# Scores of two of four batches as two float32r products over 128 rows, and P V placed with the next pair's scores

## The chip, the cores and the metric

The kernel runs on one core of one Trainium2 chip. The metric is the device time of one execution in microseconds, the median of three runs. A core has TensorE (PE in the rows, with PEld for its weight loads), VectorE (DVE), ScalarE (ACT), GpSimd (POOL) and SyncE, whose queue (SP, SPq) issues the transfers between HBM and the on-chip SBUF. TensorE writes into PSUM, in banks of 128 x 512 float32.

## What is computed

Block-causal attention for 4 batches, 8 heads, 576 tokens and a head size of 64, then two MLPs over the 2304 tokens: 512 to 1536 (a gate and a value) to 512, and 512 to 2048 to 512.

```python
scores = scale * np.matmul(q, k.transpose(0, 1, 3, 2))
mask = block_i >= block_j          # blocks of 64 tokens
scores = np.where(mask, scores, -1000000000.0)
attn = np.exp(scores - np.max(scores, axis=-1, keepdims=True))
attn = attn / (np.sum(attn, axis=-1, keepdims=True) + 1e-09)
x = np.matmul(attn, v)             # heads side by side: 2304 x 512
x = (1.0 / (1.0 + np.exp(-(x @ w_gate))) * (x @ w_val)) @ w_out
h = x @ w_in
out = np.maximum(0.01 * h, h) @ w_out2
```

## The kernel before

**The plan.** The kernel first collects all operations in a `Plan`: each has an engine, a cost, a due time, the tokens that it reads and writes, and the buffers that it uses. `order()` then simulates the engines with these costs. Whenever an engine is free it takes, of the operations whose inputs and buffers are there, the one that is due first; on TensorE an operation of the same `kind` as the last one counts as due 1.0 earlier (`GAIN`). The result is one program order for each engine. On the chip each engine, the SP queue too, works strictly in that order and waits by semaphore. Buffers come from `Ring`s: the n-th tile of a ring with k buffers waits until tile n-k has had all its users, and the tiles of a ring are taken in order.

**Float32 from float32r.** The MLP products and their weights are split: a value is its rounded copy in float32r (hi) and the rest (lo), and a product is the three products hi hi, hi lo, lo hi (line 930, and line 833 in the pair units). The score products (line 346) and P V (line 515, and line 465 for the last 64 queries) are plain float32 products.

**Attention** goes by pairs of heads, four pairs a batch. One tile `tqk` holds q and k of two heads, head a in rows 64a to 64a+63. A score product contracts over the 64 rows of one head (`sc<-qk`, 64x128 to 64x512 in the profile). Query tiles 0 and 1 come together, then tile 2, tile 3, and in the end the last 64 queries (`last_queries`, 288 keys a product, tile `sc`, two heads in the two halves of PSUM's rows). Each is followed by `softmax` (VectorE, ScalarE), by transposes on TensorE (`tp`, lines 493 and 451), and by P V: one product group for 512 queries (line 515, into `pa`) and one for the last 64 (line 465). `split` then copies the result and its rest into the activations `x` (batch 3: into `acc3`). P V is due 5.2 after its scores' due time.

**Stages.** Batch 0's attention runs alone; then the MLPs of batch 0 beside the attention of batch 1; then the MLPs of batch 1 beside the attention of batches 2 and 3, up to 615.88 us in the profile; then the MLPs of batches 2 and 3 together. The first two batches work by half units: 12 products over 256 or 320 tokens (line 931). Batches 2 and 3 share `pair_unit`s: `mix` prepares sums of the two batches' activations, and a unit is seven groups of six products (line 834) for each half of the tokens. The groups go through the PSUM rings `sc`, `mm`, `pa`, `tp`, `sc`, `mm`, `tp` in this order of due times. A unit reads four weight tiles, all of the ring `w`: `ws[0]` (`w<-wd`, 512 KB, for both `sc`), `ws[2]` (`w<-ds`, for the first `mm` and the first `tp`), `ws[3]` (`w<-ds`, for `pa` and the second `mm`) and `ws[1]` (`w<-wd`, 256 KB, for the last `tp`). `ds` holds sums of weights, made in the stage before. Of the 20 pair units some follow directly on each other; between others lie y or o products (half units).

Of the kernel before, what the change touches and what calls it, by code (L numbers as in the profile page):

```python
# [30 lines left out]
ATT_PE = 31.0  # L31
SPREAD = 14.0
NPP = 7
GAIN = 1.0


def f32(ap):
    return ap.bitcast(F32)
# [50 lines left out]
class Plan:  # L89
# [34 lines left out]
    def order(self):  # L124
# [28 lines left out]
        for _ in self.ops:  # L153
            best = None
            for e, x in ready.items():
                if x:
                    s = max(free[e], min(max(r, port) if e in o.port else r for o, r in x.items()))
                    if best is None or s < best[0]:
                        best = s, e
            assert best, "no instruction can go on"  # L160
            s, e = best
            o = min((o for o, r in ready[e].items() if r <= s and (e not in o.port or port <= s)), key=lambda o: (o.due - (GAIN if o.kind and o.kind == kind else 0), o.index))
            for x in o.engines:
                del ready[x][o]
            if e == "pe":
                kind = o.kind
            cost = o.cost[o.engines.index(e)] if o.either else o.cost
# [26 lines left out]
def block_attention_then_two_mlps(  # L194
# [34 lines left out]
    r_mag = ring("mag", 2, [P, 4 * P])  # L229
    r_rnd = ring("rnd", 2, [P, 4 * P], I32)  # L230
    r_wf = ring("wf", 3, [P, 4 * P])
    r_w = ring("w", 7, [P, 2, 4 * P], F32R)
    r_g = ring("g", 5, [P, 2, S], F32R)
    r_gf = ring("gf", 4, [P, S])
    r_qk = ring("qk", 3, [P, 2, S])
    r_v = ring("v", 2, [P, 2, NKT, D])
    r_nm = ring("nm", 6, [P, 4])
    r_sm = ring("sm", 6, [P, 4])
# [88 lines left out]
    def attention(b, start, length, alone):  # L327

        weight = [0.7, 0.9, 1.0, 1.1, 0.8]
        total = H // 2 * sum(weight)
        banks = [0]
# [5 lines left out]
        def scores(products, tqk, t):  # L339
# [3 lines left out]
            def f():  # L343
                for ps, col, row, a, q0, nq, k0, nk in products:
# [3 lines left out]
                        start=True, stop=True,  # L348
                    )

            cost = 0.1 + sum(0.1 + 0.82e-3 * x[7] for x in products)
            used = list(dict.fromkeys(x[0] for x in products))
            op("pe", cost, f, [(tqk, 0), (tqk, 1)], used, [tqk, *used], t)

        def softmax(tiles, masked, t):

# [51 lines left out]
                op(("act", "pool"), (0.24 + n / 1200, 0.25 + n / 1200), f, [r], [p_tok], [r, both], t + 2.6, port=("pool",))  # L408
            return [x[:2] for x in done]

        def pair(i):
            t_p = start + 2 * length * i / H
            at = [t_p + 2 * length * sum(weight[:c]) / (H * sum(weight)) for c in range(NKT)]

            tqk, tv = r_qk.tile(), r_v.tile()
            for a in range(2):
                load(
                    tqk, lambda a=a: tqk[a * D:a * D + D], qk[b, 2 * i + a].rearrange("s d n -> d s n"),
                    D * 2 * S * 4, t_p - 9, (), [(tqk, a)],
                )  # L420
# [16 lines left out]
            def last_queries(t):  # L437
# [29 lines left out]
                                rhs=p_l[:nr, j * P + a * BLK:j * P + (a + 1) * BLK], start=j == 0, stop=j == NKT - 1,  # L467
                            )

                op("pe", NKT * 0.24, f, [(tv, 0), (tv, 1), (p_l, 0), (p_l, 1)], [px], [px, p_l, tv], t + 5.2)  # L470
                split(S - BLK, S, "D", t + 6, px, [px])

            def query_tiles(cs):
                t = at[cs[0]]
# [7 lines left out]
            def transposed(c, tiles, t):  # L482
# [36 lines left out]

                cost = 0.1 + sum(2 * (0.05 + 0.82e-3 * (c + 1 - max(c0, j)) * P) for j in range(c + 1))  # L520
                toks = [("pt", x, a) for x in range(c0, c + 1) for a in range(2)]
                op("pe", cost, f, [(tv, 0), (tv, 1), *toks], [(pa, c)], [pa, tv, both], t + 5.2)
                split(c0 * P, (c + 1) * P, ("C" if c0 else "A") if alone else "AC", t + 6, pa, [(pa, c)])

            for cs in ([0, 1], [2], [3]):
                query_tiles(cs)
            last_queries(at[NKT - 1])

        for i in range(H // 2):
            pair(i)  # L530
# [465 lines left out]
    held, sl = {}, []  # L996
    sums_x = None

    def g_place(t, view, i=0, more=()):
        places["g"].append((view, [[(t, "g", i, hl, half) for half in range(2)] for hl in range(2)], [t, *more]))  # L1000

    def new_places():
        for t in [r_g.tile() for _ in range(5)] + [r_qk.tile(F32R) for _ in range(3)]:
            g_place(t, lambda t=t: t[:])
        g_place(sums_x, lambda: sums_x[:, 12 * S:14 * S].rearrange("p (l n) -> p l n", l=2))
# [10 lines left out]
    for n, (u, half) in enumerate(order):  # L1016
# [12 lines left out]
        if paired(u):  # L1029
# [4 lines left out]
            if u[0] == "h" and len(sl) < 3:  # L1034
                sl.append(r_sg.tile(F32R))
                for i in range(2):
                    t = sl[2]
                    g_place(t, lambda i=i, t=t: t[:, 2 * i * S:2 * (i + 1) * S].rearrange("p (l n) -> p l n", l=2), i)
                rest = r_raw.tile(F32R)
                g_place(sl[2], lambda: Parts(sl[2][:, 4 * S:], rest[:, :S]), 2, [rest])  # L1040
# [66 lines left out]
```

## Time and profile before

| | |
|---|---|
| runs, us | 1037.52, 1038.70, 1039.23 (median 1038.7) |
| the profiled execution's own time | 1036.62 |
| its span | 1034.6 |
| granted clock of TensorE | 0.998 |

The span is the time from the first to the last instruction of the profiled execution; its own time has 2.0 us more around it. Lines in the rows are those of the kernel before; tiles are named without their numbers, `out<-in`, and shapes are partitions x elements.

### The profile page before, as it was taken

What the parts mean: (1) busy time and instruction counts of PE and PEld (TensorE: products, weight loads), DVE (VectorE), ACT (ScalarE), POOL (GpSimd) and SP (SyncE); (2) the same over time, 40 slices, a digit from 0 to 9 for tenths busy, and PEclk for the clock granted to TensorE, in tenths of its full rate; (3) what the DMA queues carried; (4) which work ended last, traced back from release to release, by engine and by line L of the source; (5) the groups of instructions that cost most, each with busy time, mean ns of one, the idle gap of its engine ahead of it and who ended that gap; (6) DMA issues with size and microseconds to landing.
All of it is one profiled execution on the core that took longest, in us unless ns stands there. A gap on an engine that the chain in (4) does not pass through costs nothing.

```text
span 1034.6 us, 20242 instructions
## 1 busy us (share of the span) xinstructions
PE 1016.8 (98%) x7680; PEld 941.3 (91%) x7680; DVE 719.6 (70%) x1776; ACT 531.6 (51%) x1185; POOL 161.2 (16%) x175
## 2 busy tenths in 40 slices
PE   7899999999999999999999999999999999999998
PEld 4579898999999888889888989999999999999998
DVE  6999899999877877468556548760854887163652
ACT  6888887687748464545655534242220454331320
POOL 2331121212221414114211102110200110000000
PEclk9999999999999999999999999999999999999999
DMA  8667988679767977566755445452451435241422
GB/s 232 220 223 260 315 284 272 219 247 316 263 236 242 306 271 240 195 191 204 228 200 194 130 163 188 144 181 99 157 166 62 154 108 188 72 163 65 163 80 92
DMA packets 69984, 200.02 MB, mean 193 GB/s; under 512 B 6912, under 2 KB 16128, under 8 KB 69888
## 3 DMA queue, kind: packets, MB, share of 16 engines
q1 hardware_dynamic: 69888, 198.73, 57.4%
q8 instruction: 61, 1.00, 0.4%
q14 instruction: 35, 0.29, 0.1%
HBM read 137.36 MB, written 61.34 MB: 192 GB/s over the span
## 4 chain that ended last, share of the span: by engine, by line
PE 90%; DVE 4%; DMA 3%; ACT 2%; issue 1%; SPq 0%; ACTq 0%; DVEq 0%
PE mm L931 56%; PE mm L834 6%; PE tp L834 6%; PE sc L834 6%; PE sc L346 4%; PE pa L834 3%; PE tp L493 3%; PE pa L515 2%; DMA raw<-in_w 1%; DMA w<-wd 1%; PE tp L465 1%; PE tp L451 1%; DVE both L369 1%; PE mm L515 1%; DVE both L293 1%; ACT both L384 1%
## 5 line engine op out<-in xcount | busy, mean ns | idle before, releaser
L931 PE MATMUL mm<-g,w 128*128 128x256 f32 (+1 forms) x1776 | 271.5, 298 | 0.0
L931 PE MATMUL mm<-x,w 128*128 128x256 f32 (+1 forms) x1920 | 270.4, 298 | 0.7 <-DVE gf L958 0.7
L931 PEld LDWEIGHTS mm<-x,w 128*128 128x128 f32 x1920 | 256.7, 188 | 13.3 <-issue 6.2
L931 PEld LDWEIGHTS mm<-g,w 128*128 128x128 f32 x1776 | 246.0, 189 | 9.9 <-issue 1.9
L984 DVE TENSOR_TENSOR acc<-mm,acc 128x256 f32<-128x256 f32 (+1 forms) x160 | 72.6, 454 | 91.4 <-PE mm L931 90.5
L384 ACT ACTIVATE both<-both,nm 128x128 f32<-128x128 f32 (+2 forms) x144 | 83.0, 578 | 35.7 <-DVE nm L369 35.0
L634 POOL TENSOR_TENSOR wf<-mag,rnd 128x512 int32<-128x512 int32 x38 | 51.3, 1351 | 194.3 <-DVE mag L628 108.9
L834 PE MATMUL sc<-x,w 128*128 128x256 f32 (+1 forms) x480 | 76.3, 295 | 1.0 <-ACT v L291 1.0
L369 DVE CUSTOM_DVE_ANT_0 both<-sc,mask 128x256 f32<-128x256 f32 (+3 forms) x133 | 59.2, 478 | 24.8 <-PE sc L346 24.5
L346 PE MATMUL sc<-qk 64*64 64x288 f32 (+4 forms) x356 | 68.8, 465 | 7.0 <-DMA qk<-in_qk 5.5
L304 DVE TENSOR_TENSOR g<-gf,g 128x576 fp32r<-128x576 f32 (+2 forms) x92 | 62.5, 684 | 16.9 <-ACT g L291 16.7
L931 PE MATMUL mm<-sg,w 128*128 128x320 f32 (+1 forms) x416 | 70.2, 294 | 0.0
L834 PEld LDWEIGHTS sc<-x,w 128*128 128x128 f32 x480 | 67.8, 188 | 1.2 <-ACT v L291 1.2
L931 PE MATMUL mm<-qk,w 128*128 128x320 f32 (+1 forms) x384 | 66.8, 296 | 0.0
L402 ACT ACTIVATE both<-both,r 128x128 f32<-128x128 f32 (+4 forms) x97 | 52.9, 580 | 26.0 <-DVE r L397 25.7
L291 ACT ACTIVATE g<-gf 128x576 fp32r<-128x576 f32 (+2 forms) x72 | 42.4, 593 | 35.8 <-POOL gf L886 17.4
L931 PEld LDWEIGHTS mm<-sg,w 128*128 128x128 f32 x416 | 60.5, 188 | 0.0
L404 POOL TENSOR_SCALAR both<-both,r 128x256 f32<-128x256 f32 (+4 forms) x47 | 33.2, 711 | 153.7 <-DVE r L397 118.7
L931 PEld LDWEIGHTS mm<-qk,w 128*128 128x128 f32 x384 | 56.6, 189 | 0.0
L620 ACT ACTIVATE mag<-raw 128x512 f32<-128x512 f32 x68 | 45.7, 671 | 19.6 <-DMA raw<-in_w 14.8
L493 PE MATMUL tp<-ident,both 128*128 128x128 f32 x320 | 48.5, 282 | 3.9 <-ACT both L402 3.3
L493 PEld LDWEIGHTS tp<-ident,both 128*128 128x128 f32 x320 | 38.0, 144 | 11.4 <-ACT both L402 6.4
(169 smaller groups left out, 1610.7 us busy)
## 6 DMA issues: line engine op xcount, KB each, us to landing
w<-wd SPq DMA_DIRECT2D x116, 512.0 KB, 4.2
raw<-in_w SPq DMA_DIRECT2D x68, 512.0 KB, 4.7
wd<-w SPq DMA_DIRECT2D x68, 512.0 KB, 4.1
ds<-raw SPq DMA_DIRECT2D x40, 512.0 KB, 3.9
w<-ds SPq DMA_DIRECT2D x40, 512.0 KB, 5.8
qk<-in_qk SPq DMA_DIRECT2D x32, 288.0 KB, 5.2
v<-in_v SPq DMA_DIRECT2D x32, 160.0 KB, 3.8
w<-wd SPq DMA_DIRECT2D x20, 256.0 KB, 3.3
```

What stands on the lines that cost most here:

```text
L291: nc.scalar.activation(dst(), src(), AF.Copy)
L304: engines[e].tensor_tensor(dst(), a(), f32(b()), ALU.subtract)
L346: nc.tensor.matmul(ps[row:row + nq, col:col + nk], lhsT=tqk[half, 0, q0:q0 + nq], rhs=tqk[half, 1, k0:k0 + nk], start=True, stop=True,)
L369: nc.vector.tensor_tensor_reduce(out=pt[:, n:n + width], in0=ps[:, col:col + width], in1=mask[:, 4 * P - width:] if masked else mask[:, :w ...
L384: nc.scalar.activation(pt[:, :n], pt[:, :n], AF.Exp, bias=nm[:, k - 1:k], scale=-1.0, accum_out=sm[:, i:i + 1],)
L402: nc.scalar.activation(pt[:, :n], pt[:, :n], AF.Copy, scale=r[:, i:i + 1])
L493: nc.tensor.transpose(tp[:, (j * m + k) * P:(j * m + k + 1) * P], tiles[a][0][:, j * P:(j + 1) * P], ident)
L620: op("act", c_act(n), lambda: nc.scalar.activation(mag[:], words(1).bitcast(F32), AF.Abs), [raw], [mag], [raw, mag], d - 8)
L634: engines[e].tensor_tensor(wf[:].bitcast(I32), mag[:].bitcast(I32), rnd[:], ALU.add)
L834: nc.tensor.matmul(p[:, :n], lhsT=wt[:, wl, col + k * P:col + (k + 1) * P], rhs=srcs[k][0]()[:, xl, hs], start=k == 0 and wl + xl == 0, st ...
L931: nc.tensor.matmul(ps[:, :n], lhsT=ws[:, wl, k * P:(k + 1) * P], rhs=srcs[k]()[:, xl, hs], start=k == 0 and wl + xl == 0, stop=k == 3 and ...
L984: op("dve", c_dve(n), lambda: nc.vector.tensor_tensor(a, ps[:, :n], a, ALU.add), [ps], toks_a, [ps], e)
```

## The change

Three things change. For batches 2 and 3 (`stacked`) each head gets its own tile, filled by `halves`: q and k of one head are loaded twice, into rows 0 to 63 and 64 to 127. `hi` is the float32r copy of all of it; then q's part in the lower half is replaced by q minus its copy, so that the 128 rows hold q_hi over q_lo; `lo`, from a new ring of two tiles, holds k minus its copy in both halves. A score product becomes two float32r products over 128 rows: with k_hi (which gives q_hi k_hi + q_lo k_hi) and with `lo`. For the last queries the product of head 1 takes 128 columns of q and so writes 128 rows of PSUM, of which the lower 64 count; head 0's product then overwrites rows 0 to 63. The last queries come first in a pair. Second, P V is due when the next pair starts, and together with the remaining float32 scores it has the kind "h"; the planner counts "h" after "h" as due 6.0 earlier and adds 0.1 or 0.2 to the cost of an operation that changes between "h" and another kind. Third, the ring `w` has 6 buffers for 7, and places for results in the pair stage (`g_place`) are taken from other tiles.

```diff
-GAIN = 1.0
+GAIN = {"t": 1.0, "h": 6.0}
+TURN = {True: 0.1, False: 0.2}
...
             if e == "pe":
+                if (o.kind == "h") != (kind == "h"):
+                    cost += TURN[o.kind == "h"]
                 kind = o.kind
...
-    r_w = ring("w", 7, [P, 2, 4 * P], F32R)
+    r_w = ring("w", 6, [P, 2, 4 * P], F32R)
...
+    r_lo = ring("lo", 2, [P, S], F32R)
...
+        stacked = b >= 2
...
+            if stacked:
+                def f():
+                    for ps, col, row, a, q0, nq, k0, nk in sorted(products, key=lambda x: -x[2]):
+                        hi, lo = tqk[a]
+                        for k in range(2):
+                            nc.tensor.matmul(
+                                ps[:row + nq, col:col + nk], lhsT=hi[:, 0, q0 - row:q0 + nq],
+                                rhs=lo[:, k0:k0 + nk] if k else hi[:, 1, k0:k0 + nk], start=not k, stop=bool(k),
+                            )
...
+        def halves(head, t):
+            x, hi, lo = r_qk.tile(), r_qk.tile(F32R), r_lo.tile()
+            for half in range(2):
+                load(
+                    x, lambda half=half: x[half * D:half * D + D], qk[b, head].rearrange("s d n -> d s n"),
+                    D * 2 * S * 4, t - 12, (), [(x, half)],
+                )
+            loaded = [(x, 0), (x, 1)]
+            copy(2 * S, lambda: hi[:], lambda: x[:], loaded, [(hi, 0), (hi, 1)], [x, hi], t - 5)
+            op("dve", c_dve(S), lambda: nc.vector.tensor_tensor(
+                hi[D:, 0], x[D:, 0], f32(hi[D:, 0]), ALU.subtract
+            ), loaded, [(hi, 0)], [x, hi], t - 4, port=True)
+            sub(S, lambda: lo[:], lambda: x[:, 1], lambda: hi[:, 1], [*loaded, (hi, 1)], [lo], [x, hi, lo], t - 4)
+            return hi, lo
...
+            t_end = 0.0 if alone else t_p + 2 * length / H
...
-            tqk, tv = r_qk.tile(), r_v.tile()
-            for a in range(2):
+            if stacked:
+                tqk, tv = [halves(2 * i + a, t_p) for a in range(2)], r_v.tile()
+            else:
+                tqk, tv = r_qk.tile(), r_v.tile()
+            for a in range(0 if stacked else 2):
...
-                op("pe", NKT * 0.24, f, [(tv, 0), (tv, 1), (p_l, 0), (p_l, 1)], [px], [px, p_l, tv], t + 5.2)
-                split(S - BLK, S, "D", t + 6, px, [px])
+                op("pe", NKT * 0.24, f, [(tv, 0), (tv, 1), (p_l, 0), (p_l, 1)], [px], [px, p_l, tv], max(t + 5.2, t_end), kind="h")
+                split(S - BLK, S, "D", max(t + 5.2, t_end) + 0.8, px, [px])
...
-                op("pe", cost, f, [(tv, 0), (tv, 1), *toks], [(pa, c)], [pa, tv, both], t + 5.2)
+                op("pe", cost, f, [(tv, 0), (tv, 1), *toks], [(pa, c)], [pa, tv, both], max(t + 5.2, t_end), kind="h")
...
+            if stacked:
+                last_queries(at[0])
             for cs in ([0, 1], [2], [3]):
                 query_tiles(cs)
-            last_queries(at[NKT - 1])
+            if not stacked:
+                last_queries(at[NKT - 1])
```

The order of TensorE in the stage of batch 1's MLP, at the end of a pair of batch 2, before the change (L931 are MLP products, L346 scores, L493 transposes, L515 P V; each row is a run of like instructions):

```order
L346 MATMUL sc<-qk 128x512 x2
L931 MATMUL mm<-g,w 128x256 x12
L493 MATMUL tp<-ident,both 128x128 x6
L931 MATMUL mm<-g,w 128x320 x12
L931 MATMUL mm<-g,w 128x256 x12
L493 MATMUL tp<-ident,both 128x128 x8
L931 MATMUL mm<-g,w 128x320 x12
L515 MATMUL pa<-both,v 64x512 x2
L515 MATMUL pa<-both,v 64x384 x2
L515 MATMUL pa<-both,v 64x256 x2
L515 MATMUL pa<-both,v 64x128 x2
L346 MATMUL sc<-qk 64x288 x4
```

and around the end of a pair there after the change (L981 MLP products, L367 stacked scores with `lo` the rest of k, L562 P V):

```order
L981 MATMUL mm<-x_117,w 128x256 x12
L562 MATMUL pa<-both,v 64x512 x2
L562 MATMUL pa<-both,v 64x384 x2
L562 MATMUL pa<-both,v 64x256 x2
L562 MATMUL pa<-both,v 64x128 x2
L367 MATMUL sc<-qk 128x288
L367 MATMUL sc<-lo,qk 128x288
L367 MATMUL sc<-qk 128x288
L367 MATMUL sc<-lo,qk 128x288
L367 MATMUL sc<-qk 64x288
L367 MATMUL sc<-lo,qk 64x288
L367 MATMUL sc<-qk 64x288
```

Before, the 512-column scores, and the last queries' with P V, stand apart among MLP products; after, P V stands right ahead of the next pair's first scores, which are products of 128 rows.

The order of TensorE in two pair units that follow directly on each other, before the change, from the fourth group of a second half to the fourth of the next unit's first half (`w_8174` and `w_8317` are `ws[3]` of the two units):

```order
L834 MATMUL tp_8375<-x1_114,w_8136 128x320 x6
L834 MATMUL sc_8383<-x0_113,w_8094 128x320 x6
L834 MATMUL mm_8393<-x1_114,w_8174 128x320 x6
L834 MATMUL tp_8404<-both_7968,w_8267 128x320 x6
L834 MATMUL sc_8415<-x0_113,w_8277 128x256 x6
L834 MATMUL mm_8423<-both_7968,w_8299 128x256 x6
L834 MATMUL pa_8434<-both_7968,w_8317 128x256 x6
L834 MATMUL tp_8442<-x1_114,w_8299 128x256 x6
```

and after (`w_8466` and `w_8602` are `ws[3]`):

```order
L884 MATMUL tp_8576<-x1_117,w_8370 128x320 x6
L884 MATMUL sc_8584<-x0_116,w_8334 128x320 x6
L884 MATMUL mm_8594<-x1_117,w_8466 128x320 x6
L884 MATMUL tp_8605<-both_8147,w_8487 128x320 x6
L884 MATMUL sc_8614<-x0_116,w_8500 128x256 x6
L884 MATMUL mm_8624<-both_8147,w_8518 128x256 x6
L884 MATMUL tp_8635<-x1_117,w_8518 128x256 x6
L884 MATMUL pa_8643<-both_8147,w_8602 128x256 x6
```

The group `pa`, the first to read `ws[3]`, stood second behind the unit's first `sc` and stands behind `tp` now.

The order of SP's loads for such units, before (`w_8299` and `w_8317` are `ws[2]` and `ws[3]` of one unit, `w_8401` its `ws[1]`):

```order
L281 DMA w_8277<-wd12_135 128x1024
L281 DMA w_8299<-ds6_197 128x2x512
L281 DMA w_8317<-ds6_197 128x2x512
L281 DMA w_8401<-wd13_136 128x2x256
L281 DMA w_8411<-wd14_137 128x1024
L281 DMA w_8432<-ds7_198 128x2x512
L281 DMA w_8450<-ds7_198 128x2x512
```

and after:

```order
L287 DMA w_8500<-wd12_138 128x1024
L287 DMA w_8518<-ds6_200 128x2x512
L287 DMA w_8602<-ds6_200 128x2x512
L287 DMA w_8621<-wd13_139 128x2x256
L287 DMA w_8633<-wd14_140 128x1024
L287 DMA w_8651<-ds7_201 128x2x512
L287 DMA w_8736<-ds7_201 128x2x512
```

The loads themselves stand in the same order (`ws[0]`, `ws[2]`, `ws[3]`, `ws[1]`); with six buffers each now waits for the tile six places ahead of it in this order, where it was seven.

## Rows read from the trace of the kernel before

**Rows 1.** The profile page: busy time, share of the span and instructions of each engine.
```profile
...
PE 1016.8 (98%) x7680; PEld 941.3 (91%) x7680; DVE 719.6 (70%) x1776; ACT 531.6 (51%) x1185; POOL 161.2 (16%) x175
...
```

**Rows 2.** Stretches: start:end length, PE, PEld, DVE, ACT, POOL busy; granted clock, DMA share, GB/s.
```profile
...
26.00:52.00 26.00, 22.84 (x170) 14.15 (x168) 25.06 (x85) 22.51 (x60) 9.24 (x10) 0.93 0.69 218
315.59:615.88 300.29, 299.38 (x2290) 263.27 (x2289) 190.77 (x491) 169.31 (x384) 62.27 (x74) 1.00 0.64 215
640.00:1030.00 390.00, 390.00 (x2942) 390.00 (x2942) 221.22 (x502) 113.86 (x254) 20.34 (x25) 1.00 0.38 129
...
```

**Rows 3.** Timeline of PE, 649.3 to 653.6: start, length, what, how many.
```profile
...
649.47 1.04 PE L834 MATMUL sc<-x,w 128*128 128x320 f32 x6
650.35 1.04 PE L834 MATMUL mm<-x,w 128*128 128x320 f32 x6
...
652.81 0.87 PE L834 MATMUL mm<-both,w 128*128 128x256 f32 x6
653.52 0.28 PE L834 MATMUL pa<-both,w 128*128 128x256 f32 x1
```

**Rows 4.** Timeline of PE, 359.9 to 373.
```profile
...
360.13 4.85 PE L931 MATMUL mm<-x,w 128*128 128x256 f32 x36
364.91 0.92 PE L346 MATMUL sc<-qk 64*128 64x384 f32 x4
365.76 5.21 PE L931 MATMUL mm<-x,w 128*128 128x320 f32 x36
370.81 0.82 PE L493 MATMUL tp<-ident,both 128*128 128x128 f32 x6
...
```

**Rows 5.** The chain that ended last, 315 to 420: start, time on the chain.
```profile
...
315.66 0.86 PE sc L346 x8
...
337.03 0.66 PE tp L493 x6
...
371.62 1.06 PE sc L346 x4
...
380.12 1.12 PE sc L346 x8
...
```

**Rows 6.** Groups by form of VectorE, 315.59 to 615.88.
```profile
...
L304 DVE TENSOR_TENSOR g<-gf,g 128x576 fp32r<-128x576 f32 x16 | 14.5, 904 | 10.1 <-ACT g L291 10.1
...
L293 DVE CAST raw<-raw 128x1024 fp32r<-128x1024 f32 x7 | 4.8, 688 | 0.4 <-POOL raw L668 0.3
...
```

**Rows 7.** The tile qk, 315.59 to 615.88: ten loads of 288 KB.
```profile
...
DMA to landing us min/median/max: 3.8/4.3/8.2
```

**Rows 8.** Waits of PE over the span: total, times, longest.
```profile
...
PE sc L834 <- ACT v L291: 1.0, 1, 1.0
...
```

**Rows 9.** Single loads of the tile w, five short stretches: form, start, us to landing.
```profile
...
L281 SPq DMA_DIRECT2D w<-wd x1: 517/517/517, 649.7 to 649.7; - x1
...
DMA to landing us min/median/max: 3.7/3.7/3.7
...
L281 SPq DMA_DIRECT2D w<-ds x1: 517/517/517, 651.4 to 651.4; - x1
...
DMA to landing us min/median/max: 6.1/6.1/6.1
...
L281 SPq DMA_DIRECT2D w<-ds x1: 518/518/518, 652.3 to 652.3; - x1
...
DMA to landing us min/median/max: 6.5/6.5/6.5
...
L281 SPq DMA_DIRECT2D w<-ds x1: 518/518/518, 715.9 to 715.9; - x1
...
DMA to landing us min/median/max: 4.1/4.1/4.1
...
L281 SPq DMA_DIRECT2D w<-ds x1: 524/524/524, 629.2 to 629.2; - x1
...
DMA to landing us min/median/max: 4.7/4.7/4.7
```

More of the change, by code (lines that the diff above doesn't have):

```diff
@@ L161, in order @@
             s, e = best
-            o = min((o for o, r in ready[e].items() if r <= s and (e not in o.port or port <= s)), key=lambda o: (o.due - (GAIN if o.kind and o.kind == kind else 0), o.index))
+            o = min((o for o, r in ready[e].items() if r <= s and (e not in o.port or port <= s)), key=lambda o: (o.due - (GAIN[kind] if o.kind and o.kind == kind else 0), o.index))
             for x in o.engines:
                 del ready[x][o]
+            cost = o.cost[o.engines.index(e)] if o.either else o.cost
             if e == "pe":
+                if (o.kind == "h") != (kind == "h"):
+                    cost += TURN[o.kind == "h"]
                 kind = o.kind
-            cost = o.cost[o.engines.index(e)] if o.either else o.cost
             free[e] = s + cost
@@ L349, in f @@
                     )
+            used = list(dict.fromkeys(x[0] for x in products))
+            if stacked:
[7 more added lines that the diff above has]
+                            )
+                kinds = {}
+                cost = sum(2 * c_mm(x[7]) for x in products)
+                heads = list(dict.fromkeys(x[3] for x in products))
+                reads = [x for a in heads for x in ((tqk[a][0], 0), (tqk[a][0], 1), tqk[a][1])]
+                op("pe", cost, f, reads, used, [*used, *[x for a in heads for x in tqk[a]]], t, kind=kinds.get("last"))
+                return
             cost = 0.1 + sum(0.1 + 0.82e-3 * x[7] for x in products)
-            used = list(dict.fromkeys(x[0] for x in products))
-            op("pe", cost, f, [(tqk, 0), (tqk, 1)], used, [tqk, *used], t)
+            op("pe", cost, f, [(tqk, 0), (tqk, 1)], used, [tqk, *used], t, kind="h")
         def softmax(tiles, masked, t):
@@ L521, in transposed @@
                 toks = [("pt", x, a) for x in range(c0, c + 1) for a in range(2)]
-                op("pe", cost, f, [(tv, 0), (tv, 1), *toks], [(pa, c)], [pa, tv, both], t + 5.2)
-                split(c0 * P, (c + 1) * P, ("C" if c0 else "A") if alone else "AC", t + 6, pa, [(pa, c)])
+                op("pe", cost, f, [(tv, 0), (tv, 1), *toks], [(pa, c)], [pa, tv, both], max(t + 5.2, t_end), kind="h")
+                split(c0 * P, (c + 1) * P, ("C" if c0 else "A") if alone else "AC", max(t + 5.2, t_end) + 0.8, pa, [(pa, c)])
+            if stacked:
+                last_queries(at[0])
             for cs in ([0, 1], [2], [3]):
                 query_tiles(cs)
-            last_queries(at[NKT - 1])
+            if not stacked:
+                last_queries(at[NKT - 1])
         for i in range(H // 2):
@@ L997, in block_attention_then_two_mlps, with g_place @@
     sums_x = None
-    def g_place(t, view, i=0, more=()):
-        places["g"].append((view, [[(t, "g", i, hl, half) for half in range(2)] for hl in range(2)], [t, *more]))
+    def g_place(ts, view, i=0):
+        places["g"].append((view, [[(ts[0], "g", i, hl, half) for half in range(2)] for hl in range(2)], ts))
     def new_places():
         for t in [r_g.tile() for _ in range(5)] + [r_qk.tile(F32R) for _ in range(3)]:
-            g_place(t, lambda t=t: t[:])
-        g_place(sums_x, lambda: sums_x[:, 12 * S:14 * S].rearrange("p (l n) -> p l n", l=2))
+            g_place([t], lambda t=t: t[:])
+        los = [r_lo.tile(), r_lo.tile()]
+        g_place(los, lambda: Parts(los[0][:], los[1][:]))
+        g_place([sums_x], lambda: sums_x[:, 12 * S:14 * S].rearrange("p (l n) -> p l n", l=2))
         for i in range(NKT):
@@ L1037, in block_attention_then_two_mlps @@
                     t = sl[2]
-                    g_place(t, lambda i=i, t=t: t[:, 2 * i * S:2 * (i + 1) * S].rearrange("p (l n) -> p l n", l=2), i)
-                rest = r_raw.tile(F32R)
-                g_place(sl[2], lambda: Parts(sl[2][:, 4 * S:], rest[:, :S]), 2, [rest])
+                    g_place([t], lambda i=i, t=t: t[:, 2 * i * S:2 * (i + 1) * S].rearrange("p (l n) -> p l n", l=2), i)
                 mix(False, due[u, half] - 14)
```

## The prediction

> **What bounds the kernel now.** I read the page first, then the busy time by stretches, then the waits, and only then single instructions and loads. The span is 1034.6 us and TensorE is busy for 98% of it [rows 1]. By stretches [rows 2]: while batch 0's attention runs alone, TensorE is busy for 22.84 of 26 us and VectorE for 25.06, so there VectorE sets the pace. From 315.59 to 615.88, where batch 1's MLP runs beside the attention of batches 2 and 3, TensorE is busy for 299.38 of 300.29 us, VectorE for 190.77, ScalarE for 169.31, at a granted clock of 1.00 (the 2.4 GHz level). From 640 to 1030 TensorE is busy for all 390.00 us. So in the stretch that the change is about, whatever shortens TensorE's own work shortens the kernel, work that is added to VectorE and ScalarE is covered, and so are loads, up to the point where a product has to wait for one.
>
> The profiled execution takes 1036.62 us, 2.0 more than its span and 2.1 less than the median of 1038.7. I forecast the difference and add it to the median. A difference within 0.2%, 2.1 us, is about what a measurement of this kernel can't tell from no change.
>
> **What the score products cost.** Six full-tile products of 320 columns take 0.88 us (649.47 to 650.35), six of 256 take 0.71 (652.81 to 653.52) [rows 3]: 0.147 and 0.118 each, 0.45 ns a column. By that line 288 columns cost 0.132, 384 cost 0.175, 512 cost 0.232, and 128 cost 0.061. The last is an extrapolation; the nearest row of that width are transposes, 0.66 for six, 0.110 each [rows 5]. Between 0.061 and 0.110 I take 0.10, as the transposes have the same tile and as many columns. A pair of heads now issues 4 products each of 128, 256, 384 and 512 columns and 8 of 288: 0.40 + 0.47 + 0.70 + 0.93 + 1.06 = 3.56 us (3.40 to 3.60). Before, the first two tiles take 0.86, the last queries 1.12, the 512 columns 1.06 [rows 5], and the 384 columns 0.85 (364.91 to 365.76) [rows 4]: 3.89. That saves 0.33 a pair, **-2.6 us** for eight pairs (-2.3 to -3.9).
>
> The Trainium skill (TensorE: Matmul & The Clock Gate, sections Back-to-back issue gap and LDWEIGHTS) has a stream of loads and products of 128 columns at about 81 ns each and one load of 128 columns at about 107 ns, longer than such a product: it speaks against the extrapolated 61 ns, as the transposes' 110 ns do. By 81 ns the four products would take 0.32 a pair and the saving would be 3.3 us.
>
> **What the changes of tile cost.** The old score products and both P V products use a part of the array. Around the score block at 364.91 the 36 full-tile products ahead take 4.78 us (360.13 to 364.91), where 24 of 0.118 and 12 of 0.147 make 4.59; those behind take 5.05 (365.76 to 370.81) where it should be 4.94 [rows 4]. That is 0.30 for leaving the full tile and coming back; each run has a transpose group at its other end, which takes up to 0.1 of it. I take 0.20 an excursion. Counted in the order that the program fixes for TensorE, there are 34 excursions in this stretch before: four to five a pair, as the two small tiles, the 384, the 512, the last queries with P V behind them, and the last queries' own P V stand apart. After, the scores fill all 128 rows, P V stands right ahead of the next pair's scores, and 16 are left: 18 x 0.20 = **-3.6 us**. Head 0's last-query products write only 64 rows of PSUM; if that still counts as a part of the array, seven excursions come back (+1.4); no row shows such a shape, so I take half, **+0.7**. Batch 1's attention keeps its products, but its P V moves too: 19 to 15 excursions there, **-0.8**. In batch 0's stretch VectorE paces, and 4 fewer excursions are worth nothing that I can name; a changed order there can give or cost 1.5.
>
> **What the new preparation costs.** Each head now takes two q and k loads instead of one, a copy of 1152 elements a row and two subtractions of 576. VectorE's subtraction of 128x576 takes 0.90 in this stretch, its copy of 1024 elements 0.69 [rows 6]: at most 2 x 0.90 + 0.77 = 2.6 a head, 5.1 a pair, 41 us in all, if no copy goes to ScalarE. That fits: 190.77 + 41 is 232 of 300 us. What can be late is the chain of the pair's second head: it gets its buffer when the last 512-column score of the pair before is done, then loads (landing 4.3, at worst 8.2 [rows 7]), copies and subtracts (2.6), some 7 to 11 us. In the new order 13 us or more of other products lie between that score and the next pair's first one. VectorE works in order, and one of its long operations can stand ahead; I allow 0.1 a pair, **+0.8**. A score product that waits there holds all products behind it on TensorE, the MLP's among them.
>
> The mixing of batches 2 and 3 ahead of the pair units makes TensorE wait once, 1.0 us for a ScalarE copy [rows 8]. The last P V now stands between earlier products; half of this wait may go: **-0.5** (0 to -1.0).
>
> **What the sixth buffer costs.** The ring of weight buffers goes from 7 to 6. In the stage of pair units the loads go out in bursts, each when a product has freed a buffer. With seven, the `w<-ds` that the product `pa` reads goes out third or fourth in a burst, a unit early, and its landing after 6.1 or 6.5 us [rows 9] holds nobody up. With six it can go out only when the unit before is done with its own `w<-ds` for `mm` and `tp`, which is behind that unit's fourth product of the second half, and then it is first in its burst; the planner has also moved `pa` behind `tp` in such a unit. From there to `pa` lie three products of 320 columns (3 x 0.88) and three of 256 (3 x 0.71): 4.76 us, less 0.2 for the release (649.47 to 649.7 [rows 3, 9]). So the load must land in 4.56. Of 20 units 13 follow directly on another pair unit and have this condition; ahead of the others y or o products lie between. A `w<-ds` load alone lands in 4.1, one with a store just behind it in 4.7, one third in a burst in 6.1; a 256 KB load that is first of four lands in 3.7 [rows 9], so those behind delay the first only a little. I take 4.7, a stall of 0.14: 13 x 0.14 = **+1.8 us**. The bounds are 0 (4.1) and 13 x 1.54 = 20 (6.1). Behind a waiting `pa` all products of the unit wait, and the loads that they release with them, so a stall isn't caught up.
>
> The Trainium skill (DMA: Bandwidth & Descriptors, Rules for kernel authors) says that two transfers that one engine issues use the same ring on each of 16 DMA engines and serialize. By that the first of a burst lands as if alone and the term is 0. The trace agrees only in part: the third and the fourth of the burst are issued 0.9 apart and land 1.3 apart, but both much later than a load alone.
>
> **Sum.** Scores -2.6, changes of tile -3.6 + 0.7 - 0.8, chain +0.8, mixing -0.5, sixth buffer +1.8: -4.2 us. 1038.7 - 4.2 = **1034.5 us**.
>
> **Rivals.** *The sixth buffer takes it back* (slower). Without its term the sum is -6.0 us; with a stall of 0.46 in each of 13 units, a landing after 5.0, nothing is left, and from 5.2 on it is slower by over 0.2%. At 5.4 the time is 1038.7 - 6.0 + 13 x 0.84 = 1043.6, at the 6.1 of a third load 1052.7. For it: the 4.7 where only one store follows. Against it: the 3.7 of the smaller load with three behind it.
>
> *The gain is absorbed* (about the same). The second head's chain comes 0.5 late in each of eight pairs (+3.2 on my allowance), and the narrow products count as a change of tile (+0.7): 1034.5 + 3.9 = 1038.4. For it: a landing of 8.2 has happened [rows 7], and a subtraction takes 0.90. Against it: VectorE idles for a third of the stretch.
>
> *More than forecast.* Products of 128 columns at 0.061 (-1.3), no stall at the sixth buffer (-1.8), no cost of the narrow ones (-0.7): 1030.7.
>
> **How the numbers follow.** My forecast, with a range of its own from 1032 to 1036.5, has 0.42, more than that 0.12, the absorbed case 0.22, the sixth buffer 0.24. Faster by over 0.2%: 0.42 + 0.12 = 0.54; same 0.22; slower 0.24. The range for 8 in 10 leaves out the lowest part of the third rival and the upper half of the first: 1030 to 1045.
>
> **What would show it.** Right: the stretch that ended at 615.88 ends about 6 us earlier with VectorE at some 215 to 230 us; stacked products of 256 columns start 0.118 apart; no wait of the stacked scores for `lo` or `qk` over 0.5; in the stage of pair units `pa` waits for DMA `w<-ds` for under 3 us in total, and TensorE is busy for nearly all of it. Wrong: waits of `pa` for `w<-ds` of 0.5 or more in 13 places (the sixth buffer); waits of scores for VectorE in each pair (absorbed); stacked products that start further apart than full-tile ones of the same width; an opening that is longer by over 1.5 us.

## The result and the profile after

The changed kernel takes 1044.12 us (median of 12 runs), the kernel before 1039.04 in the same comparison: a ratio of 1.0053, 95% interval 1.0035 to 1.0071. It is slower by 0.5%, and its runs scatter more: 1040.7 to 1048.7, where eleven of the twelve before lie from 1037.4 to 1042.9 (one took 1979.92 and is left out of the ratio). The profiled execution after took 1045.62 us, 9.0 more than the profiled one before, and its span of 1043.8 is 9.2 longer. The medians lie only 5.1 apart, so what follows shows where the time goes, and its sums are some 4 us larger than the usual difference.

Where the time is lost shows in the stretches of the changed kernel (start:end, length, busy time of PE, PEld, DVE, ACT, POOL, granted clock, DMA share, GB/s). The first begins with the first stacked product and ends with the first pair unit's product:

```profile
...
313.39:623.78 310.39, 300.20 (x2290) 281.11 (x2289) 214.99 (x527) 178.41 (x398) 64.31 (x75) 0.98 0.69 225
640.00:1030.00 390.00, 389.97 (x2934) 388.66 (x2934) 226.08 (x514) 116.77 (x261) 21.15 (x26) 1.00 0.38 128
...
```

In [rows 2] the like stretch was 300.29 us long with 0.9 us of idle TensorE. Now it is 10.1 longer: TensorE idles for 10.2 us, and is busy for as long as before although it has less to do, at a mean clock of 0.98. The stretch starts 2.2 us earlier than before (313.39 against 315.59), and what lies behind it takes 1.3 us more (420.0 against 418.7). The stage of pair units is as full as it was. VectorE is busy for 215 us in the first stretch, within the 215 to 230 that I had forecast, so the amount of added work is no larger than I took it to be.

The waits of TensorE in this stretch are mostly not waits of the new score products, but of transposes (L540). These wait for copies and subtractions by VectorE and ScalarE: `both` holds the softmax results and their transposes, `x` the activations (total, times, longest):

```profile
...
PE tp L540 <- DVE both L299: 3.2, 2, 2.0
PE tp L540 <- DVE x L310: 2.8, 4, 1.6
PE sc L367 <- DVE nm L395: 1.0, 2, 0.7
PE sc L367 <- DVE lo L310: 0.8, 1, 0.8
PE sc L367 <- DVE qk L447: 0.8, 1, 0.8
...
```

The chain that ended last tells why a transpose waits. This is its piece behind the 512-column scores (L367) that end at 484.43:

```profile
...
484.43 3.53 PE mm L981 x24
...
487.98 0.33 SPq L287
...
488.36 0.60 SPq L287
...
489.01 9.03 DMA qk<-in_qk
...
498.14 1.18 ACT qk L297
...
499.35 1.09 DVE qk L447
...
500.47 0.57 DVE both L299
...
501.17 0.56 PE tp L540 x3
...
```

To be read from the end: the transposes at 501.17 waited for a VectorE copy of an earlier transpose's result (`both`), which stood in VectorE's queue behind the subtraction of q (L447), which waited for ScalarE's copy of q and k, which waited for the load. The load started 4.6 us after the scores that free its buffer had ended, and landed 9.03 later. SP's queue shows what stood ahead of it (start, time of the group, how many):

```profile
...
483.95 1.33 SPq L287 DMA_DIRECT2D qk<-in_qk  x2
486.22 2.09 SPq L287 DMA_DIRECT2D w<-wd  x2
488.36 1.25 SPq L287 DMA_DIRECT2D qk<-in_qk  x2
```

Two weight loads, each waiting for MLP products to free a weight buffer, hold the second head's loads. All 28 loads of q and k in this stretch land in

```profile
...
DMA to landing us min/median/max: 4.1/6.3/9.0
```

where the median was 4.3 [rows 7]. From the end of a pair's 512-column scores to the landing of the next pair's last load it is 8.5 to 13.6 us (333.6 to 345.3, 371.0 to 381.7, 409.7 to 421.8, 448.5 to 459.5, 484.4 to 498.0, 522.1 to 530.5, 557.7 to 569.1). The copy and the subtractions come behind that, and mostly 13 to 16 us lie between these scores and the next pair's first ones (522.1 to 535.1, 409.7 to 426.0; once 18, and 21 with the stall in it).

### The profile page after: what moved, and what is told of

Its sections match the earlier page's. It is cut to its first block, busy times and chain, and to the rows that moved or that the text cites. A ratio compares the mean times of both kernels' runs of the same rounds, so it can differ in the third digit from the quotient of the medians.

```text
span 1043.8 us, 20258 instructions
## 1 busy us (share of the span) xinstructions
PE 1016.4 (97%) x7680; PEld 957.7 (92%) x7680; DVE 744.7 (71%) x1810; ACT 540.7 (52%) x1197; POOL 160.9 (15%) x177
## 4 chain that ended last, share of the span: by engine, by line
PE 69%; DVE 14%; DMA 7%; ACT 6%; issue 2%; SPq 1%; POOL 0%; ACTq 0%; DVEq 0%; POOLq 0%
PE mm L981 39%; PE tp L884 6%; PE mm L884 6%; PE sc L884 6%; DMA qk<-in_qk 4%; PE pa L884 3%; PE sc L367 2%; PE tp L540 2%; DMA raw<-in_w 2%; PE pa L562 2%; DVE mag L678 1%; ACT both L410 1%; DVE w L310 1%; DVE both L395 1%; DVE g L310 1%
## 5 line engine op out<-in xcount | busy, mean ns | idle before, releaser
L981 PE MATMUL mm<-x,w 128*128 128x256 f32 (+1 forms) x1920 | 270.2, 298 | 0.1
L981 PE MATMUL mm<-g,w 128*128 128x256 f32 (+1 forms) x1752 | 266.3, 298 | 0.3 <-DVE w L310 0.2
L981 PEld LDWEIGHTS mm<-x,w 128*128 128x128 f32 x1920 | 258.5, 189 | 5.7 <-issue 1.7
L981 PEld LDWEIGHTS mm<-g,w 128*128 128x128 f32 x1752 | 243.9, 190 | 3.8 <-issue 0.9
L410 ACT ACTIVATE both<-both,nm 128x256 f32<-128x256 f32 (+4 forms) x144 | 82.9, 578 | 37.4 <-DVE nm L395 37.2
L395 DVE CUSTOM_DVE_ANT_0 both<-sc,mask 128x384 f32<-128x384 f32 (+4 forms) x133 | 59.7, 478 | 15.3 <-PE sc L367 7.6
L684 POOL TENSOR_TENSOR wf<-mag,rnd 128x512 int32<-128x512 int32 x34 | 45.9, 1350 | 157.6 <-DVE mag L678 84.6
L430 POOL TENSOR_SCALAR both<-both,r 128x384 f32<-128x384 f32 (+4 forms) x53 | 36.2, 688 | 183.2 <-DVE r L423 145.6
L981 PE MATMUL mm<-sg,w 128*128 128x256 f32 (+1 forms) x384 | 64.2, 296 | 0.0
L540 PE MATMUL tp<-ident,both 128*128 128x128 f32 x320 | 49.4, 285 | 13.3 <-DVE both L299 3.2
L981 PE MATMUL mm<-qk,w 128*128 128x256 f32 (+1 forms) x360 | 62.2, 296 | 0.0
L540 PEld LDWEIGHTS tp<-ident,both 128*128 128x128 f32 x320 | 37.4, 144 | 22.9 <-issue 5.2
L428 ACT ACTIVATE both<-both,r 128x512 f32<-128x512 f32 (+4 forms) x91 | 48.8, 575 | 14.9 <-DVE r L423 14.7
L981 PEld LDWEIGHTS mm<-sg,w 128*128 128x128 f32 x384 | 56.0, 190 | 0.0
L981 PEld LDWEIGHTS mm<-qk,w 128*128 128x128 f32 x360 | 52.9, 189 | 0.0
L310 DVE TENSOR_TENSOR w<-wf,w 128x512 fp32r<-128x512 f32 x68 | 48.0, 706 | 1.5 <-ACT w L297 1.4
```

Source lines behind the costliest of these rows:

```text
L310: engines[e].tensor_tensor(dst(), a(), f32(b()), ALU.subtract)
L395: nc.vector.tensor_tensor_reduce(out=pt[:, n:n + width], in0=ps[:, col:col + width], in1=mask[:, 4 * P - width:] if masked else mask[:, :w ...
L410: nc.scalar.activation(pt[:, :n], pt[:, :n], AF.Exp, bias=nm[:, k - 1:k], scale=-1.0, accum_out=sm[:, i:i + 1],)
L428: nc.scalar.activation(pt[:, :n], pt[:, :n], AF.Copy, scale=r[:, i:i + 1])
L430: nc.gpsimd.tensor_scalar(out=pt[:, :n], in0=pt[:, :n], scalar1=r[:, i:i + 1], scalar2=0.0, op0=ALU.mult, op1=ALU.add)
L540: nc.tensor.transpose(tp[:, (j * m + k) * P:(j * m + k + 1) * P], tiles[a][0][:, j * P:(j + 1) * P], ident)
```

## The experiments

Theory 1: a q,k load that lands late holds the preparation (the copy and the subtractions of q and k), and with it the softmax operations behind it in ScalarE's and VectorE's queues, and so the transposes. Theory 2: the sixth weight buffer does it. Theory 3: P V at the next pair's start leaves the softmax less room. All runs below are compared with the kernel before on their own chip, in several rounds; across chips it is the ratios that compare.

**Nothing waits for the landing.**

```diff
+            def same(n, rows=slice(0, P)):
+                return ident[rows, :64].unsqueeze(1).broadcast_to([rows.stop - rows.start, n, 64])
...
-            sub(S, lambda: lo[:], lambda: x[:, 1], lambda: hi[:, 1], [*loaded, (hi, 1)], [lo], [x, hi, lo], t - 4)
+            sub(S, lambda: fold(lo[:]), lambda: same(9), lambda: fold(hi[:, 1]), [*loaded, (hi, 1)], [lo], [x, hi, lo], t - 4)
```

(The copy and the other subtraction are changed in the same way; `ident` is a constant tile, and `fold` only splits the columns into groups of 64.)

> The changed kernel in its own order on every engine, with the same loads, but the copies and subtractions that prepare q and k read a constant tile instead of the loaded one, so nothing waits for a q or k load of batches 2 and 3 to land (the scores' values are left out by this). Theory 1 (a q,k load that lands late holds the copies and subtractions, and the softmax work behind them on ScalarE and VectorE, and so the transposes on TensorE): nearly all of the 16 us of added stalls between 313 and 624 go, time 1030 to 1034. Theory 2 (the sixth weight buffer makes the stalls there): 1041 to 1044. Theory 3 (P V at the next pair's start leaves the softmax less room): 1040 to 1044.

Measured: 1034.76, ratio 0.9959 (0.9946 to 0.9972), 9.4 us less than the changed kernel in its own order and with the same loads. Its stretch from the first stacked product to the first pair unit's product:

```profile
...
314.39:611.94 297.55, 294.63 (x2291) 277.18 (x2289) 214.53 (x527) 178.85 (x398) 64.12 (x75) 1.00 0.72 234
...
```

VectorE and ScalarE are as busy as in the changed kernel, idle TensorE is down from 10.2 to 2.9 us, and TensorE's busy time from 300.2 to 294.6. The stretch is 12.8 us shorter; some of that is lost again behind it, where 422.6 us follow instead of 420.0. So the loss is the wait for the landing, not the work of the preparation, and not the place of P V.

**The planner is told of the landing.**

```diff
...
-                    D * 2 * S * 4, t - 12, (), [(x, half)],
+                    D * 2 * S * 4, t - 12, (), [(x, half)], lat=6.0,
...
```

(The planner counts about 0.9 us for the issue and then 1.8 to the landing; `lat` replaces the 1.8.)

> The changed kernel, but the planner counts 6.0 us instead of 1.8 from the end of a q,k load's issue to its landing for batches 2 and 3, so that it puts the preparation later in the order of ScalarE and VectorE. Theory 1: fewer operations stand behind a late load, the added stalls fall by half or more, 1033 to 1039. Theories 2 and 3: nothing that they name changes, 1042 to 1046.

Measured: 1036.57, ratio 0.9981 (0.9966 to 0.9996). One number in the plan is worth 7.5 us.

**A seventh buffer in the same order, and its control.**

```diff
-    r_w = ring("w", 6, [P, 2, 4 * P], F32R)
+    r_w = ring("w", 7, [P, 2, 4 * P], F32R)
+    r_w.bufs = 6
...
-        raw, mag, rnd = r_raw.tile(), r_mag.tile(), r_rnd.tile()
+        raw, mag, rnd = r_raw.tile(), r_mag.tile(), wf
...
```

> The changed kernel with a seventh weight buffer on the chip while the planner still counts six, so that the order in the stage of batch 1's MLP is the same and only waits for a free buffer shrink; the space comes from the integer tiles of the weight conversion, which use the tile of its result instead (this changes a few places in the first stages). Theory 1: SP's queue frees q,k loads a little earlier behind the weight loads, 1041 to 1044. Theory 2: the stalls go, 1032 to 1037. Theory 3: 1043 to 1045.

The control keeps the second edit alone:

```diff
-        raw, mag, rnd = r_raw.tile(), r_mag.tile(), r_rnd.tile()
+        raw, mag, rnd = r_raw.tile(), r_mag.tile(), wf
```

> The kernel of the run with a seventh weight buffer, with its integer tiles of the conversion in the result's tile too, but with six weight buffers: the pair of runs differs in the seventh buffer alone, and not in the order. Theory 1 in its narrow form (only the landing of a q,k load is late): the same as with seven, 1041 to 1044. Theory 2 in the form that the seven-buffer trace suggests (weight loads that wait for a buffer hold the q,k loads behind them in SP's queue; with seven the stalls of that stage were 7 us where they were 17): 1049 to 1054, since the conversion itself loses some 10 us in the first stages.

Measured: 1042.56 with seven, ratio 1.0030 (1.0016 to 1.0043), and 1048.66 with six, ratio 1.0107 (1.0092 to 1.0123). By the ratios the seventh buffer is worth 0.77%, 8 us, in one and the same order; the space that was made for it costs some 5 us (1048.66 against 1044.12). Theory 1 in its narrow form missed, and the other form comes out just below its 1049: weight loads that wait for a buffer belong to the delay.

**P V's place.** First the changed kernel without its second part:

```diff
...
-            t_end = 0.0 if alone else t_p + 2 * length / H
+            t_end = 0.0
...
```

(and no kind "h" for P V and scores, so that no turn is counted).

> The changed kernel without its second part: P V is due 5.2 us after its scores again, has no kind, and the planner counts no cost for turns; stacked scores and six weight buffers stay. Theory 1: the late loads stay, some 10 changes of tile come back (+2 us), 1043 to 1048. Theory 2: 1044 to 1047. Theory 3: the stalls go and the changes of tile come back, 1033 to 1038.

Then the kernel before with this part alone, `GAIN` and `TURN` as in the change:

```diff
...
+            t_end = 0.0 if alone else t_p + 2 * length / H
...
-                op("pe", cost, f, [(tv, 0), (tv, 1), *toks], [(pa, c)], [pa, tv, both], t + 5.2)
+                op("pe", cost, f, [(tv, 0), (tv, 1), *toks], [(pa, c)], [pa, tv, both], max(t + 5.2, t_end), kind="h")
...
```

> The kernel before with the second part of the change alone: P V due when the next pair starts, kind h for it and the float32 scores, costs of turns in the planner; scores stay float32, seven weight buffers. TensorE leaves the full tile 63 times where it was 72. Theories 1 and 2 (P V's place is not the loss): 9 x 0.2 less, 1036 to 1038. Theory 3 (the place of P V makes the transposes wait): 1041 or more.

Measured: 1046.07, ratio 1.0068 (1.0046 to 1.0091), and 1034.27, ratio 0.9965 (0.9952 to 0.9978). P V's new place is a gain by itself, 3.1 us and so more than I had named, and without it the changed kernel is no faster. Theory 3 falls.

**The sixth buffer alone**, in the kernel before:

```diff
-    r_w = ring("w", 7, [P, 2, 4 * P], F32R)
+    r_w = ring("w", 6, [P, 2, 4 * P], F32R)
```

> The kernel before with six weight buffers for seven and nothing else; scores stay float32 and no q,k load of a head stands behind more weight loads than two. If the sixth buffer costs only what waits in the stage of pair units (1 to 3 us): 1038 to 1041. If six buffers hold SP's queue, and the softmax behind it, by themselves: 1042 or more. If the loss of 6 us that the seventh buffer took from the changed kernel comes only through the q,k loads of the stacked scores: 1038 to 1041 too, with no new waits of transposes before the pair units.

Measured: 1043.50, ratio 1.0046 (1.0030 to 1.0062). That is the time of my second case, not of the first. The profiled execution (1041.54) reaches the pair units 2.3 us later and takes 2.8 more from there to the end. Of the softmax that the second case names it shows little: TensorE idles for 2.0 us in the stage ahead of the pair units, where it was 0.9. In the pair units the products' own loading of weights into the array (PEld) waits for transfers that land 5.2 and 5.4 us after their issue:

```profile
...
PEld pa L834 <- DMA w<-ds: 1.6, 2, 0.9
...
```

**How the two divide.** All of the change but the stacked scores, that is, the kernel before with P V's part and

```diff
-    r_w = ring("w", 7, [P, 2, 4 * P], F32R)
+    r_w = ring("w", 6, [P, 2, 4 * P], F32R)
```

> The kernel before with P V's new place and six weight buffers, but float32 scores: it differs from the changed kernel in the stacked scores (and the places of the pair units' results) alone. If the parts add up, -3.1 for P V and +4.6 for the buffer: 1039 to 1042, and the stacked scores as planned cost the remaining 3 to 5 us. If six buffers and P V's place together hold the order as much as the changed kernel: 1043 to 1046, and the stacked scores are neutral.

Measured: 1041.88, ratio 1.0032 (1.0020 to 1.0044), my first case. The changed kernel's 1.0053 (1.0035 to 1.0071) is 0.2% more, which the two intervals don't tell from nothing: the stacked scores as planned bring no gain, and whether they cost anything isn't shown. The parts give -3.1 + 4.6 = +1.5 where +3.4 is measured, and this difference isn't clear of the intervals either. So with P V in its new place the sixth buffer costs 0.7%, some 7 us, without any stacked score. In the profiled execution 4.4 of 8.1 us more than with P V's place alone lie behind the start of the pair units, where two loads land 6.2 and 6.1 us after their issue, each first in its burst:

```profile
...
PEld pa L838 <- DMA w<-ds: 3.3, 2, 1.7
...
```

And the changed kernel with seven buffers, for which one of seven softmax rows is given up:

```diff
-NPP = 7
+NPP = 6
...
-    r_w = ring("w", 6, [P, 2, 4 * P], F32R)
+    r_w = ring("w", 7, [P, 2, 4 * P], F32R)
...
```

> The changed kernel with seven weight buffers in the planner too, with six softmax rows for seven and one place for results elsewhere; the planned landing is 2.7 as in the change. If the sixth buffer is the larger part of the loss: 1035 to 1039. If the late preparation holds the softmax with seven buffers as well: 1040 to 1045.

Measured: 1047.56, ratio 1.0079 (1.0064 to 1.0094): both cases that I named were too low. With seven buffers the late preparation holds the softmax just as it does with six. The stretch from the first stacked product to the pair units is 309.4 us long (310.4 with six), TensorE idles for 10.6 us in it and waits most for the same things:

```profile
...
318.72:628.16 309.44, 298.83 (x2290) 278.07 (x2289) 217.06 (x536) 177.50 (x393) 60.33 (x71) 0.99 0.70 226
...
PE tp L540 <- DVE x L310: 2.7, 2, 2.4
PE tp L540 <- ACT both L297: 2.5, 2, 1.8
...
```

What makes this kernel slower than the changed one lies ahead: its first stacked product comes at 318.72, 5.3 us later. The missing softmax row is the likely reason, which no run shows by itself; the stretch in question is not what put the time above both cases.

The same kernel with 9.0 planned for the landing,

> The planned landing of 9.0 with seven weight buffers; the space comes from one of the seven softmax rows (six stay), and the place that this takes from the pair units' results is found elsewhere. The pair units lose their waits (-1 to -3) and q,k loads go out earlier: 1029.5 to 1032, unless six softmax rows hold the scores: 1034 or more.

(`lat=9.0` in the load) takes 1034.42, ratio 0.9958 (0.9946 to 0.9970), my second case: this one number is worth some 13 us there. So the seventh buffer doesn't save the change, and the planned landing does.

**How far the planned landing goes.** Three kernels as the second experiment, with six buffers: with `lat=6.0` the loads due earlier, then `lat=9.0`, and then both, as here:

```diff
...
-                    D * 2 * S * 4, t - 12, (), [(x, half)],
+                    D * 2 * S * 4, t - 30, (), [(x, half)], lat=9.0,
...
```

> The kernel with the planned landing of 6.0 us, and the q,k loads of batches 2 and 3 due 18 us earlier, so that SP's queue takes them ahead of weight loads when both can go. If weight loads in front of them are a part of the delay: 1033 to 1036. If only the landing counts: as with the planned landing alone, 1036 to 1037.5.

> As the planned landing of 6.0 us, with 9.0, the longest that the changed kernel shows. Theory 1: ScalarE and VectorE stand behind a load even less, 1034 to 1036.5, unless the planner now puts the preparation so late that the stacked scores themselves wait for it: 1037 to 1040, with waits of the scores for lo or qk in the trace.

> The planned landing of 9.0 and the q,k loads due 18 us earlier. If both act on different parts of the delay: 1031 to 1032.5. If the planned landing leaves nothing for the earlier issue: 1032.8 as before.

Measured: 1035.00, ratio 0.9977 (0.9962 to 0.9991); 1032.81, ratio 0.9950 (0.9936 to 0.9963); 1032.68, ratio 0.9942 (0.9930 to 0.9954). Going first in SP's queue adds nothing that can be told from the planned landing, and 9.0 alone does better than either case that I had named. With 9.0 the stretch is

```profile
...
314.82:609.59 294.77, 291.22 (x2270) 275.25 (x2269) 215.11 (x528) 171.67 (x382) 71.24 (x83) 1.00 0.72 237
...
```

(the last pair's P V, 2.3 us, falls behind its end here). The loads still land late (a median of 5.5, at worst 10.3). What changed is the order: the next pair's first scores now come 23 to 29 us behind the 512-column ones (569.8 to 593.2, 415.0 to 443.0) where it was mostly 13 to 16, and the load lands in that time.

**Too far.**

```diff
...
-                    D * 2 * S * 4, t - 12, (), [(x, half)],
+                    D * 2 * S * 4, t - 12, (), [(x, half)], lat=12.0,
...
```

> As with 9.0, with 12.0 us planned. The measured landing of a second head's load is 11 to 13 us behind the 512-column score that frees its buffer, so either a little better, 1031.5 to 1033, or the planner puts the preparation so late that stacked scores wait: 1034 to 1038.

Measured: 1058.91, ratio 1.0195 (1.0182 to 1.0208). The second case, but far beyond my 1038. In the last pair the planner has put all that TensorE could do meanwhile ahead of the scores, and these wait in one piece. Within that wait the clock goes to 0.50, the 1.2 GHz level, for 17 us:

```profile
...
612.17 2.02 PE L981 MATMUL mm<-g,w 128*128 128x320 f32 x12
623.86 0.61 PE L367 MATMUL sc<-qk 128*128 128x288 f32 x1 [9.66 <-DVE qk L447]
...
617.20:634.27 17.07, 9.21 (x29) 6.90 (x29) 7.34 (x26) 5.87 (x17) 1.93 (x4) 0.50 0.24 66
...
```

The wait of 9.7 us, and half of the 9.2 us in which TensorE is busy at that level, make some 14 of the 26 us that this kernel is slower than with 9.0; the rest isn't taken apart.

## Why the prediction was wrong, step by step

*Scores* (-2.6): 1.8 of it came. The stacked products of the changed kernel by the starts of their groups:

```profile
...
536.61 0.29 PE L367 MATMUL sc<-lo,qk 128*128 128x288 f32 x1
536.74 0.29 PE L367 MATMUL sc<-qk 128*64 128x288 f32 x1
536.88 0.30 PE L367 MATMUL sc<-lo,qk 128*64 128x288 f32 x1
...
540.63 0.31 PE L367 MATMUL sc<-qk 128*128 128x128 f32 x1
...
541.11 0.33 PE L367 MATMUL sc<-qk 128*128 128x256 f32 x1
...
541.63 1.93 PE L981 MATMUL mm<-x,w 128*128 128x320 f32 x12
...
549.59 0.34 PE L367 MATMUL sc<-qk 128*128 128x384 f32 x1
...
550.29 6.52 PE L981 MATMUL mm<-x,w 128*128 128x256 f32 x48
556.65 0.39 PE L367 MATMUL sc<-qk 128*128 128x512 f32 x1
...
```

The four of 128 columns take 0.48 (0.12 each, not 0.10), those of 256 take 0.52 for 0.47, of 384 columns 0.70 as worked out, of 512 columns 0.90 (556.65 to 557.55) for 0.93, and those of 288 start 0.13 apart. That is 3.66 a pair where I had 3.56. The price of the Trainium skill (TensorE: Matmul & The Clock Gate, Back-to-back issue gap), 81 ns for 128 columns, is too low here; the transposes were the right row.

*Changes of tile* (-3.6 + 0.7 - 0.8): right together, as far as can be told. The stretch up to the pair units holds the same products before and in the run where nothing waits for a landing, both at a clock of 1.00, and TensorE is busy for 299.38 and 294.63 us. Of the 4.7 us between them the scores are 1.8, which leaves 2.9 for 18 excursions fewer, 0.16 each, and -3.6 + 0.7 was 2.9 too. The narrow products of head 0 (`128*64`) follow the full ones and each other without a gap, 0.13 to 0.14 apart from 536.61 to 536.88, so the +0.7 wasn't needed (P V's float32 products have this shape too, and there I had counted it as a part of the array), and 0.20 an excursion was somewhat high. Where P V moves alone the sign holds too, with 9 excursions fewer and 3.1 us gained, but only one of the 9 lies in that stretch; waits of transposes that went from 0.9 to 0.2 us there make 0.7, and the rest isn't traced.

*Mixing* (-0.5): the 1.0 us that TensorE waited for ScalarE's `v` [rows 8] doesn't stand among its waits any more; its weight loads wait 0.3 for it.

*The preparation* (+0.8) is the step that failed. I took the load as issued when its buffer is freed and as landing in 4.3 us, and set 7 to 11 us against 13. Measured are 2.8 to 5.5 us until the last load's issue, since weight loads stand ahead in SP's queue, and 5.7 to 9.0 to its landing: 8.5 to 13.6, and the copy and the subtractions behind. And I let the late chain cost only what the scores themselves wait for. It stands in the queues of ScalarE and VectorE, and the transposes of the pair at hand, which have nothing to do with it, wait. Without waits for the landing the time falls by 9.4 us, against my 0.8. That it falls to 1034.8, nearly what I had forecast for the whole, is in part luck: behind the start of the pair units this run takes 3.8 us more than the profiled one before, where I had 1.8. My rival of the absorbed gain named this chain, at 4.0 us in all (3.2 above my allowance); it was more than twice that.

*The sixth buffer* (+1.8): right in the stage that I looked at, in the changed kernel. The first load of a burst lands in 4.3 there (issued at 656.8), within 4.56, and the pair units' `pa` waits for it three times:

```profile
...
PEld pa L884 <- DMA w<-ds: 0.6, 3, 0.2
...
```

The Trainium skill (DMA: Bandwidth & Descriptors, Rules for kernel authors) says of two transfers to disjoint halves of the partitions that they share the 16 DMA engines, on the same rings if one engine issues them, and so serialize. This trace agrees: the first of a burst comes nearly as if alone. It isn't so every time: with six buffers and float32 scores two such loads landed after 5.2 and 5.4, and with P V's new place two after 6.2 and 6.1, which held `pa` for 1.5 us each, the price in my rival of the sixth buffer, but at two places and not at 13. And I looked at one stage. In the one before, six buffers cost the kernel before about 2 us, and the changed kernel's q,k loads stand there behind weight loads that wait for a buffer.

*Range and chances*: the 1044.1 lies within 1030 to 1045; the sign was that of the case with 0.24, for another reason than the one I gave it.

*Open*: how much of the 4.6 us of the sixth buffer is in each place, since its profiled execution is 2 us faster than its median; whether P V's place and the sixth buffer really cost 1.9 us more together than one by one; and whether a longer planned landing would help the kernel before, with P V's part, which wasn't run.

## What to carry to other kernels

A list scheduler, one that takes the operation due first whenever an engine is free, is only as good as its landing times: where an engine's order is fixed, an operation that waits for a load blocks everything behind it, so a planned landing that is too short costs the work of others. Plan what the trace shows from the freed buffer to the landing, the queue ahead of the load included, and check the plan with one run that takes the landing away and one that plans it longer. A part that gains by itself (here P V's place, 0.35%) should be timed alone before it goes together with one that needs space from a ring: the best kernel here is the changed one with 9.0 us planned, 0.5% faster than before, and most of that is P V's place. What the stacked scores add to it, with the sixth buffer that they need, is 0.15%, and the two intervals overlap.

## What the runs showed of the hardware

TensorE's clock can fall after a short idle. Around the wait at 499.2 to 501.2 in the changed kernel (stretches of 1 us; the clock is the third number from the end):

```profile
...
499.00:500.00 1.00, 0.16 (x2) 0.00 (x0) 0.66 (x1) 1.00 (x4) 0.91 (x2) 1.00 0.64 258
500.00:501.00 1.00, 0.00 (x0) 0.00 (x0) 0.97 (x2) 1.00 (x4) 1.00 (x2) 1.00 1.10 389
501.00:502.00 1.00, 0.83 (x5) 0.86 (x6) 0.93 (x4) 0.21 (x2) 0.71 (x2) 0.76 0.83 197
502.00:503.00 1.00, 1.00 (x6) 1.00 (x5) 1.00 (x3) 1.00 (x2) 0.00 (x0) 0.50 0.93 340
503.00:504.00 1.00, 1.00 (x6) 1.00 (x5) 0.79 (x3) 0.97 (x3) 0.00 (x0) 0.50 0.12 45
504.00:505.00 1.00, 1.00 (x6) 0.96 (x5) 0.84 (x2) 0.15 (x2) 0.00 (x0) 0.54 0.00 0
505.00:506.00 1.00, 1.00 (x11) 1.00 (x10) 0.81 (x3) 0.94 (x3) 0.00 (x0) 1.00 0.07 16
...
```

After 2.0 us without a product the clock goes to 0.50, the 1.2 GHz level, and stays there for some 3 us in which TensorE is busy and does half the work: 0.24 + 0.50 + 0.50 + 0.46 = 1.7 us lost on top of 2.0. A second drop, to 580, comes with waits of 0.6, 0.8 and 0.8 us and costs 3.2 in the same way:

```profile
...
572.00:574.00 2.00, 0.84 (x2) 0.47 (x2) 1.97 (x3) 0.00 (x0) 2.00 (x2) 0.80 0.11 43
574.00:576.00 2.00, 2.00 (x9) 1.73 (x9) 1.42 (x7) 1.85 (x4) 0.09 (x1) 0.50 0.00 0
576.00:578.00 2.00, 2.00 (x10) 2.00 (x9) 1.83 (x7) 1.64 (x5) 0.73 (x1) 0.50 0.00 0
578.00:580.00 2.00, 2.00 (x9) 2.00 (x9) 1.11 (x2) 0.86 (x3) 0.00 (x0) 0.50 0.65 262
...
```

So these stalls cost about twice their length and more (2.0 and 1.7, 2.2 and 3.2), and TensorE's busy time rises with them: 300.2 us in the changed kernel against 294.6 without the waits for the landing, for the same products. Not every stall does this: waits of 1.6 us at 425.7 and of 1.2 at 388.6 in the same execution, and of 2.7 at 435.5 in the run with a seventh buffer in the same order, leave the clock at 1.00.
